# A pointwise convolution streamed through one core: chunks of 2048 rows in four buffers, or of 4096 rows in three

## The chip, the core and the metric

The kernel runs on one core of one Trainium2 chip. The metric is the device time in microseconds (us) of one execution; the time of a version is the median of its runs. A profile is one execution on the chip, recorded by the hardware profiler. The engines are called PE (matmul), PEld (its weight loads), DVE (VectorE), ACT (ScalarE), POOL (GpSimd) and SP (which here only issues DMAs and waits).

## What is computed

The reference is a depthwise separable convolution with a 1 x 1 depthwise part, on an image of 384 x 384 pixels with 384 channels, all in bf16:

```python
H = W = 384; C = 384; k = 1
out = x * dw[0, 0]                        # one factor per channel
return einsum('bhwc,cd->bhwd', out, pw)   # 384 x 384 matrix
```

With one row per pixel this is a matrix product: 147,456 rows of 384 values, times a 384 x 384 matrix whose rows have been scaled by `dw`. The input and the output have 113.2 MB each.

## The kernel before

**Tiling.** The work is cut into 288 supertiles of 512 rows. Supertiles are gathered in chunks, and a chunk is what one load and one store move. `_chunks` makes chunks of 1, 1 and 2 supertiles at the start, then 70 chunks of `LMAX` = 4 supertiles (2048 rows), then 2, 1 and 1 at the end: 76 chunks. Chunk t uses input buffer `Xs[t % NX]` and output buffer `Os[t % NO]`, with four of each.

**Layout.** A load gives each of the 128 partitions 4L consecutive rows of a chunk of L supertiles, so that its run in memory is 4L x 768 bytes: 12 KB for L = 4. A supertile j of the chunk takes four of these rows per partition, L rows apart (the view `(k l)` in `transposes`). A store writes four runs per partition, one for each quarter q of the chunk, of L rows each: 3 KB for L = 4. At any L a load has one run per partition and a store four.

**One supertile.** DVE transposes its rows into `Ts` in two instructions (line 174), each over 96 pairs of channels. PE multiplies with 48 small matmuls (line 134) on four row groups into a PSUM buffer of four banks. Then the result is evicted to the output buffer with a cast to bf16: DVE takes quarter 3 (line 212) and ACT takes quarters 0 to 2 (line 215). `Ts` and the PSUM buffers are double, so supertiles alternate between two of each. The scaled weights `w_r` are made once at the start, by DVE and ACT.

**Order.** Everything is written out by hand and tied by semaphores. DVE's order in the main loop is: evict supertile jj, then transpose supertile jj + 2. PE runs a loop over pairs of supertiles. DVE waits for a chunk's load before the chunk's first transposes (`s_x`), and both DVE and ACT wait, before a chunk's first eviction, for the store that last used the output buffer (`s_o`).

**SP's queue.** All loads of x and all stores are issued on SP, in one order: the first NX loads, and then for each t, load t + NX and store t. Load t + NX waits for the last transposes of chunk t, since these free the input buffer (line 95). Store t waits for the last evictions of chunk t by DVE (line 105) and by ACT (line 107). An instruction that waits on SP holds up those behind it.

Of the kernel before, what the change touches and what calls it, by code (L numbers as in the profile page):

```python
# [9 lines left out]
U32 = mybir.dt.uint32  # L10
COPY = mybir.ActivationFunctionType.Copy

LMAX = 4
NX = 4
NO = 4


def _chunks(n_super: int):

    head, tail = [1, 1, 2], [2, 1, 1]  # L20
    mid = n_super - sum(head) - sum(tail)
    assert mid > 0 and mid % LMAX == 0
    return head + [LMAX] * (mid // LMAX) + tail


@with_exitstack
def kernel(
# [22 lines left out]

    NS = N // 512
    chunks = _chunks(NS)
    NT = len(chunks)
    s0 = [sum(chunks[:t]) for t in range(NT)]
# [11 lines left out]

    Xs = [bufp.tile([P, 4 * LMAX, C], BF16, name=f"X{i}") for i in range(NX)]
    Ts = [bufp.tile([P, NB, 256], BF16, name=f"T{i}") for i in range(2)]
    Os = [bufp.tile([P, 4 * LMAX * D], BF16, name=f"O{i}") for i in range(NO)]
    PS = [psum.tile([P, 4, 512], F32, name=f"ps{s}") for s in range(2)]  # L70

    s_x = [nc.alloc_semaphore(f"s_x{i}") for i in range(NX)]
    s_t = [[nc.alloc_semaphore(f"s_t{i}{h}") for h in range(2)] for i in range(2)]
    s_pe = nc.alloc_semaphore("s_pe")
    s_a = [nc.alloc_semaphore(f"s_a{i}") for i in range(2)]
    s_d = [nc.alloc_semaphore(f"s_d{i}") for i in range(2)]
    s_o = [nc.alloc_semaphore(f"s_o{i}") for i in range(NO)]
    s_dw = nc.alloc_semaphore("s_dw")
# [5 lines left out]
    with tc.tile_critical():  # L84
# [6 lines left out]
        def load_x(t):  # L91
            L = chunks[t]
            r = 512 * s0[t]
            src = xf[r : r + 512 * L, :].rearrange("(p s) c -> p (s c)", p=P)
            d = nc.sync.dma_start(Xs[t % NX][:, : 4 * L, :].rearrange("p s c -> p (s c)"), src)  # L95
            if t >= NX:
                je = s0[t - NX] + chunks[t - NX] - 1
                d._wait_ge(s_t[je % 2][1], je // 2 + 1)
            d.then_inc(s_x[t % NX], 16)

        def store(t):
            L = chunks[t]
            r = 512 * s0[t]
            je = s0[t] + L - 1
            nc.sync.wait_ge(s_d[je % 2], je // 2 + 2)
            dst = of[r : r + 512 * L, :].rearrange("(q p j) d -> p q (j d)", q=4, p=P)
            d = nc.sync.dma_start(dst, Os[t % NO][:, : 4 * L * D].rearrange("p (q e) -> p q e", q=4))
            d._wait_ge(s_a[je % 2], je // 2 + 2)
            d.then_inc(s_o[t % NO], 16)

# [9 lines left out]
        for t in range(NT):  # L120
            if t + NX < NT:
                load_x(t + NX)
            store(t)
        for o in range(NO):
            nc.sync.wait_ge(s_o[o], 16 * len(range(o, NT, NO)))

# [123 lines left out]
```

## Time and profile before

| | before |
|---|---|
| median of 8 runs | 588.48 us (587.54 to 590.28) |
| the profiled execution | 590.12 us, with a span of 588.3 us from its first to its last instruction |
| granted PE clock | 0.994 |
| busy in the span | PE 564.3, DVE 564.1, PEld 396.7, ACT 326.7 us |
| HBM traffic | read 114.43 MB, written 113.25 MB, 387 GB/s over the span |
| queue of SP's DMAs | 51,488 packets, 227.09 MB, 98.5% of 16 DMA engines' time |
| loads of 1.5 MB | 70, median 13.8 us from issue to landing |
| stores of 1.5 MB | 70, median 15.5 us from issue to landing |

A row of the profile's list of groups is to be read so: line, engine, operation, destination and source with shapes, the count, the busy time in us and the mean in ns of one, and at last the idle time of the engine before such instructions, with what ended most of it. "To landing" is the time from the issue of a DMA until its last byte has arrived and its semaphore is raised. It holds the time in which the DMA lies in the queue behind others. The share of the DMA engines is a mean over 16 of them.

### The profile page before, as it was taken

Reading aid. Unit: us, or ns where it says so; the run is one execution under the profiler, and the core shown is the slowest. Engines: PE = TensorE matmul, PEld = TensorE weight load, DVE = VectorE, ACT = ScalarE, POOL = GpSimd, SP = SyncE. Lnnn points to the kernel's source line nnn. Section 1 sums busy time; section 2 is a strip of 40 time slices with the busy share of each in tenths; the row PEclk is TensorE's granted clock in tenths of the full one; section 3 lists DMA queues with packets and bytes.
Section 4 is the critical chain, followed back from the end, with each engine's and each line's share of the span. In section 5 each row is a group of like instructions: output and inputs, shape, how many; then the busy total and the mean of one; then the engine's idle time right before and its main releaser. Section 6 shows DMA issues by size and latency. Waiting matters only on the chain.

```text
span 588.3 us, 30055 instructions
## 1 busy us (share of the span) xinstructions
PE 564.3 (96%) x13824; PEld 396.7 (67%) x13824; DVE 564.1 (96%) x876; ACT 326.7 (56%) x297; POOL 0.3 (0%) x5
## 2 busy tenths in 40 slices
PE   1999999999999999999999999999999999999992
PEld 0677777777777777777777777777777777777771
DVE  3899999999999999999999999999999999999991
ACT  3455555555555655555555556555555555565552
POOL 0000000000000000000000000000000000000000
PEclk9999999999999999999999999999999999999997
DMA  8999999999999999999999999999999999999974
GB/s 293 348 407 407 406 402 411 387 390 416 403 399 394 402 401 404 395 385 419 416 403 395 399 396 401 415 420 413 404 396 390 391 406 376 395 386 374 374 300 168
DMA packets 52126, 227.81 MB, mean 387 GB/s; under 512 B 2704, under 2 KB 6544, under 8 KB 43152
## 3 DMA queue, kind: packets, MB, share of 16 engines
q1 hardware_dynamic: 51488, 227.09, 98.5%
q10 hardware_dynamic: 624, 0.59, 0.4%
q14 instruction: 13, 0.11, 0.1%
q8 instruction: 1, 0.02, 0.0%
HBM read 114.43 MB, written 113.25 MB: 387 GB/s over the span
## 4 chain that ended last, share of the span: by engine, by line
PE 93%; DMA 4%; ACT 1%; SPq 0%; issue 0%; ACTq 0%
PE ps L134 93%; DMA out_dram<-O 3%; DMA pw_r<-in_pw_dram 1%; ACT w_r L199 1%; ACT O L215 0%; SPq L89 0%; SPq L95 0%; SPq L245 0%; ACTq L211 0%; ACTq L194 0%; SPq L84 0%
## 5 line engine op out<-in xcount | busy, mean ns | idle before, releaser
L134 PE MATMUL ps<-w_r,T 32*128 32x384 bf16 x13824 | 564.3, 322 | 14.1 <-ACT w_r L199 13.0
L134 PEld LDWEIGHTS ps<-w_r,T 32*128 32x128 bf16 x13824 | 396.7, 93 | 181.4 <-issue 14.5
L215 ACT CAST O<-ps 128x1152 bf16<-128x1152 f32 x288 | 322.0, 1118 | 245.8 <-PE ps L134 242.8
L174 DVE STREAM_TRANSPOSE T<-X 128x384 uint32<-128x384 uint32 x576 | 448.0, 853 | 1.5 <-PE ps L134 1.4
L212 DVE CAST O<-ps 128x384 bf16<-128x384 f32 x288 | 160.7, 558 | 7.1 <-PE ps L134 5.0
L199 ACT ACTIVATE w_r<-pw_r,dwsel 128x384 bf16<-128x384 bf16 x6 | 3.1, 601 | 5.7 <-DMA pw_r<-in_pw_dram 5.7
L186 DVE CAST dwsel<-dwt 32x12 f32<-32x12 bf16 x4 | 0.7, 164 | 3.7 <-DMA dwt<-in_dw_dram 3.6
L197 DVE TENSOR_SCALAR w_r<-pw_r,dwsel 128x384 bf16<-128x384 bf16 x6 | 1.5, 312 | 2.6 <-DMA pw_r<-in_pw_dram 2.6
L160 ACT ACT_TABLE_LOAD x1 | 1.3, 1283 | 2.3 <-issue 2.3
L157 DVE MEMSET seed<- 128x1 f32 x2 | 0.1, 59 | 1.0 <-SPq L84 1.0
L160 ACT COPY warm<-warm 128x1 f32<-128x1 f32 x2 | 0.3, 188 | 0.0
L234 POOL MEMSET const-uint8-127<- 128x1 uint8 x1 | 0.1, 102 | 0.0
L234 POOL MEMSET const-bfloat16-1.0<- 128x1 bf16 x1 | 0.1, 101 | 0.0
L158 POOL MEMSET warm<- 128x3 f32 x1 | 0.1, 100 | 0.5 <-SPq L84 0.5
L234 POOL MEMSET const-float32-0.0<- 128x1 f32 x1 | 0.1, 98 | 0.2 <-issue 0.2
L234 POOL MEMSET const-float32-1.0<- 128x1 f32 x1 | 0.1, 98 | 0.0
## 6 DMA issues: line engine op xcount, KB each, us to landing
X<-in_x_dram SPq DMA_DIRECT2D x70, 1536.0 KB, 13.8
out_dram<-O SPq DMA_DIRECT2D x70, 1536.0 KB, 15.5
X<-in_x_dram SPq DMA_DIRECT2D x4, 384.0 KB, 11.6
X<-in_x_dram SPq DMA_DIRECT2D x2, 768.0 KB, 14.9
out_dram<-O SPq DMA_DIRECT2D x4, 384.0 KB, 7.0
out_dram<-O SPq DMA_DIRECT2D x2, 768.0 KB, 9.8
pw_r<-in_pw_dram ACTq DMA_DIRECT2D x2, 288.0 KB, 5.9
pw_r<-in_pw_dram SPq DMA_DIRECT2D x2, 288.0 KB, 6.6
```

Of the source, the lines that this page charges most:

```text
L134: mm = nc.tensor.matmul(PS[s][:, q, :D], lhsT=Ts[s][32 * q : 32 * q + 32, b, par::2], rhs=w_r[32 * q : 32 * q + 32, b, par, :], start=(b = ...
L157: nc.vector.memset(seed[:, s : s + 1], 0.0).then_inc(s_d[s])
L158: nc.gpsimd.memset(warm[:], 0.0).then_inc(s_seed)
L160: c = nc.scalar.copy(warm[:, s + 1 : s + 2], warm[:, 0:1])
L174: ins = nc.vector.transpose(out=Tw[:, 3 * h : 3 * h + 3], in_=Xw[:, :, j, 96 * h : 96 * h + 96].rearrange("p k (b w) -> p b k w", w=32),)
L186: nc.vector.tensor_copy(dwsel[32 * q : 32 * q + 32, :], dwt[:].rearrange("w b r -> w (b r)")).then_inc(s_ds)
L197: i = nc.vector.tensor_scalar_mul(w_r[:, b, r, :], pw_r[:, b, r, :], sc)
L199: i = nc.scalar.activation(w_r[:, b, r, :], pw_r[:, b, r, :], COPY, scale=sc)
L212: e = nc.vector.tensor_copy(Ov[:, 3, j, :], PS[s][:, 3, :D])
L215: a = nc.scalar.copy(Ov[:, 0:3, j, :], PS[s][:, 0:3, :D])
L234: nc = _bacc.Bacc("TRN2", target_bir_lowering=False, num_devices=1)
```

## The change

Chunks become twice as large and buffers fewer: `LMAX` goes from 4 to 8, so that a chunk has 4096 rows, and there are three input and three output buffers in place of four. One more step of 4 supertiles is put into the start and the end, so the chunks are 1, 1, 2, 4, then 34 of 8, then 4, 2, 1, 1: 42 chunks. A full load has 3 MB with a run of 24 KB per partition, and a full store has four runs of 6 KB per partition. The buffers of each kind hold 24 supertiles together, where they held 16.

```diff
-LMAX = 4
-NX = 4
-NO = 4
+LMAX = 8
+NX = 3
+NO = 3
 
 def _chunks(n_super: int):
 
-    head, tail = [1, 1, 2], [2, 1, 1]
+    head, tail = [1, 1, 2, 4], [4, 2, 1, 1]
     mid = n_super - sum(head) - sum(tail)
     assert mid > 0 and mid % LMAX == 0
     return head + [LMAX] * (mid // LMAX) + tail
```

On PE, DVE and ACT the instructions and their order stay as they are, with other buffers behind them. On SP there are 42 loads of x and 42 stores in place of 76 and 76. Load t + 3 now follows the freeing of chunk t's buffer, where it was load t + 4.

## The prediction

> **What bounds the kernel now.** I read the page's costliest groups first, then the timeline around one supertile (512 rows), then the landing times of the DMAs in stretches, and last the stretches at the end. The groups name two full engines:
>
> ```profile
> L134 PE MATMUL ps<-w_r,T 32*128 32x384 bf16 x13824 | 564.3, 322 | 14.1 <-ACT w_r L199 13.0
> L174 DVE STREAM_TRANSPOSE T<-X 128x384 uint32<-128x384 uint32 x576 | 448.0, 853 | 1.5 <-PE ps L134 1.4
> L212 DVE CAST O<-ps 128x384 bf16<-128x384 f32 x288 | 160.7, 558 | 7.1 <-PE ps L134 5.0
> ```
>
> PE's ends are modelled, so its 564.3 decides nothing. DVE's columns are busy total, mean ns, idle before: with 1.5 and 7.1 us of idle in all, DVE runs without a gap. The timeline gives its beat:
>
> ```profile
> 27.34 0.56 DVE L212 CAST O<-ps 128x384 bf16<-128x384 f32 x1
> 27.34 1.12 ACT L215 CAST O<-ps 128x1152 bf16<-128x1152 f32 x1 [0.83 <-PE ps L134]
> 27.81 1.55 DVE L174 STREAM_TRANSPOSE T<-X 128x384 uint32<-128x384 uint32 x2
> 29.29 0.56 DVE L212 CAST O<-ps 128x384 bf16<-128x384 f32 x1
> ```
>
> One eviction and two transposes, 29.29 - 27.34 = 1.95 us per supertile. Supertile 0's pair, before PE had started, took 1.54 us too, so this is DVE's own time. Eviction j starts at 21.49 + 1.95 (j - 2), so the last (287) is due at 577.24. It started at 579.38. The loss is at the end, and the DMAs make it. Loads, columns as in the page (issue durations min/median/max; then us to landing), in the stretches 50 to 100, 450 to 500 and 500 to 540 us:
>
> ```profile
> L95 SPq DMA_DIRECT2D X<-in_x_dram x7: 328/328/328, 52.8 to 99.6; - x7
> DMA to landing us min/median/max: 8.2/9.3/9.7
> ...
> L95 SPq DMA_DIRECT2D X<-in_x_dram x7: 328/349/1176, 450.6 to 497.4; - x7
> DMA to landing us min/median/max: 18.4/18.8/19.9
> ...
> L95 SPq DMA_DIRECT2D X<-in_x_dram x5: 328/2825/3951, 505.2 to 536.4; - x5
> DMA to landing us min/median/max: 20.6/22.1/22.3
> ```
>
> Same transfers, same spacing, and each lands later: a backlog grows. From 100-150 (median 10.6) to 450-500 (18.8) it is 8.2 us in 350, or 0.18 us per chunk of 7.8: the DMAs need 7.98 us where DVE takes 7.8. It is one engine of the 16 (columns: DVE and ACT busy, granted clock, DMA share, GB/s):
>
> ```profile
> 568.00:570.00 2.00, 2.00 (x56) 1.40 (x52) 2.00 (x5) 1.17 (x2) 0.00 (x0) 1.00 0.22 85
> 570.00:571.00 1.00, 1.00 (x33) 0.69 (x25) 1.00 (x2) 0.55 (x1) 0.00 (x0) 1.00 0.07 25
> 583.00:584.00 1.00, 0.00 (x0) 0.00 (x0) 0.00 (x0) 0.00 (x0) 0.00 (x0) 0.50 0.07 25
> ```
>
> A share of 0.07 is one sixteenth. At 570 fifteen engines have finished everything issued, and one still works on a load (issued 559.79, landing 15.4 later at 575.2) and a store (562.78, landing 16.5 later at 579.3). The transposes of supertile 287 start at 575.33, with that load (the view names PE for it). The last eviction starts at 579.38, with that store.
>
> **What can be won.** Without backlog: last ScalarE eviction 577.24 + 1.12 = 578.4, a store like the first one (3.7 us to landing) 582.1, and the 1.3 us from the last landing (580.5 + 6.5 = 587.0) to the span's end: 583.4. So of the span of 588.3 at most 4.9 us can go. The rest is DVE's beat: the change issues the same 864 compute instructions on DVE in the same order, and leaves ScalarE's and PE's order alone. X is read at another stride (row groups 6 KB apart, not 3 KB). Supertile 0 (768 B apart) took 1.54 us a pair and the others 1.55, so I cost it at nothing.
>
> **Part by part.**
> *DMA count and run length.* 76 loads and 76 stores become 42 and 42; on each DMA engine, 8 load runs of 12 KB and 32 store runs of 3 KB per 2048 rows become 8 of 24 KB and 32 of 6 KB per 4096. What a run costs shows at the end, where the slow engine is alone: stores land at 579.3, 583.0, 584.9, 585.9 with 98.3, 49.2 and 24.6 KB per engine for the last three intervals. 3.7 - 1.0 us for 73.7 KB more is 27.3 GB/s, and 1.0 us less 24.6 KB at that rate leaves 0.1 us for 32 runs: about 3.1 ns a run. Twenty runs saved per 7.8 us are 0.06 us. The backlog's growth falls from 0.18 to 0.12 per 2048 rows, 0.24 per new chunk; 34 chunks give 8.2 us.
> Is more saved? 3.146 MB at 16 x 27.3 GB/s are 7.20 us, so 0.78 us per pair of DMAs are above it. If that sits at the turn from load to store and back, the change halves it (-0.39 us, no backlog at all); if it goes with the bytes on that one engine, only the 0.06 is saved. Bounds 0.06 to 0.39, and none if longer runs bring a cost of their own. I take 0.06: at 570, without turns and without other engines, the one engine moved 25 GB/s, so most of its slowness goes with bytes.
> Two rules of the Trainium skill, page "DMA: Bandwidth & Descriptors", stand against the rows. Section "Where 436 GB/s comes from" says that for HBM to SBUF transfers the HBM side binds at about 358 GB/s. By it longer runs can't help and this kernel would take 227.8 MB / 358 = 636 us; the page shows 387 to 420 GB/s in most slices, so I drop it. Section "Anatomy of one DMA" fits some 2.0 us fixed per DMA (for the other issue path): 68 fewer DMAs would save 136 us. The row allows 0.78 us for two, since queued DMAs overlap, and all but 4.9 us is behind DVE anyway.
> *Slack.* A load is issued when its buffer's last transposes end, and needed NX - 1 chunks on: 3 x 7.8 = 23.4 us before, 2 x 15.6 = 31.2 after. The new load itself takes some 7.3 us and the store 8.5, so base landing times rise by about 7.5, the same as the slack. No stall in mid-run unless the backlog passes about 12 us. On SP a load that waits for its buffer has that chunk's own store behind it, which waits for evictions two supertiles later anyway, so the longer wait holds nothing up.
> *Head.* Before, loads 4 (issued 7.0), 5 (18.72) and 6 (21.59) fed supertiles 8 to 19. Now chunk 4 (supertiles 8 to 15, 3 MB) waits for chunk 1's buffer and, on SP, behind the first store: issue 18.7. Its rows are due at 29.76. Before, half of it took 8.4 us to land (27.1); load 4 of the same size landed 3.6 us after load 3. So 27.1 + 3.6 = 30.7, a stall of 1.0 us. Bounds: 0 (if the slow 8.4 was a start effect) to 4.3 (both halves slow). I take 1.0. It moves all of DVE's work.
> *Tail.* The last load (supertile 287) now waits for chunk 38's transposes, issued at about 567.6 instead of 559.8, and lies in SP's queue and the rings behind the 3 MB store of chunk 37, issued 562.8. Queue empty by then: first packet about 1.5 us after issue, 8.5 for the store on the slow engine, 0.9 for the load: 573.7, due at 573.8. No stall, no reserve. The store of chunk 38 (570.6) follows at +4.3 = 578.0; its buffer is due at 577.24: 0.8 us. Is the queue empty? In the two chunk periods before 562.8 the loads are 1.5, 0.8 and 0.4 MB instead of 3 and 3: 3.6 + 4.6 = 8.2 us are given back against 8.2 of backlog. It just is.
> *Sum.* Last eviction 577.24 + 1.0 + 0.8 = 579.0, ScalarE 580.2, last store 4.0 (it follows small ones), 1.3: span 585.5, 2.8 under 588.3. The profiled execution took 590.12, 1.8 around its span; the median of 588.48 is 1.6 lower, so an ordinary run probably has a little less tail to win. I take 2.5: 586.0.
>
> **Rivals.**
> *Forecast, 0.47: 586.0.*
> *The turns were the cost, 0.12: 584.3.* Growth gone, tail wait gone, only the head's 1.0 left: 583.4 + 1.0, which is 3.9 under the span, 0.3 less for the median. For it: loads alone at 11 to 18 us ran at 393 to 449 GB/s. Against it: 25 GB/s at 570 without turns.
> *Gain given back, 0.16: 588.5.* Between 500 and 540 the landing rose 3.3 us more, beyond the steady growth, with 360 to 385 GB/s. If such a patch comes again, the queue isn't empty at 562.8 but 3.3 behind, and the last load is late by that much: 585.5 + 3.3 = 588.8, half a us over the span, which the median's smaller tail takes back.
> *Slower, 0.25: 591.3.* The last load behind the 3 MB store. If longer runs save the slow engine nothing, 0.36 us per chunk x 34 = 12.2, less 8.2 given back, leaves 4.0, or 7.3 with such a patch; each us delays the last transposes one for one: span 589.5 to 592.8, the middle 2.9 over the span before. It decides from a remainder of 2.8 us. For it: the reserve there is 0.1 us, where the old tail issued that load 7.8 us earlier. Against it: the 3.1 ns per run.
> About 0.2% is what can be told from no change here: faster 0.59, same 0.16, slower 0.25. The range: 583.6 (all 4.9 us) to 592.0 (most of the slower case).
>
> **What would show it.** Transposes still 853 ns and evictions 1.95 us apart; load landings rising from about 15 by 5 to 8 us, not by 14; a DVE idle of about 1 us before supertile 8 at 30 us; the last load issued near 568 and landing near 574 to 576; a last eviction near 579. It is wrong if landings rise past 30 us (waits on stores in mid-run, slower), if they don't rise at all (second case), or if the head stalls by 3 us or more.

## The result, and the profile after

The changed kernel takes 586.82 us (median of 22 runs, 585.83 to 587.37) where the kernel before takes 588.21 (59 runs). The ratio is 0.9969 (95% interval 0.996 to 0.9977), that is 1.8 us of 588; the two medians are 1.4 apart. The forecast was 586.0, 2.5 us less than before. Ratios here and below are of fast runs alone: three of the 22 runs of e3, its profiled execution among them, are slow, at 596.8 us and more with a granted clock of 0.987 to 0.989. The profiled execution took 585.49 with a span of 583.7, which is at the fast end: the other runs have spans of 583.1 to 585.6, most near 585.0.

DVE's beat of 1.95 us is as it was. The landing times of the loads are not. The same view as before (issue durations min/median/max on SP, then us to landing), for the stretches 100 to 150, 450 to 500 and 500 to 530 us of the changed kernel:

```profile
L95 SPq DMA_DIRECT2D X<-in_x_dram x3: 327/328/328, 107.6 to 138.8; - x3
DMA to landing us min/median/max: 15.3/15.5/15.7
...
L95 SPq DMA_DIRECT2D X<-in_x_dram x4: 327/328/328, 450.8 to 497.6; - x4
DMA to landing us min/median/max: 19.2/19.4/19.5
...
L95 SPq DMA_DIRECT2D X<-in_x_dram x2: 327/328/328, 513.2 to 528.8; - x2
DMA to landing us min/median/max: 16.1/17.8/19.6
```

Two things are to be seen. The landing rises by 3.9 us in 350, or 0.17 per chunk of 15.6 us, where it had risen 0.18 per 7.8: the growth is halved. And after 500 there is no jump: the full load issued at 513.2 lands after 19.6 us, where before the change the median rose to 22.1. (The load at 528.8, 16.1, is already one of half the size.) The middle number of the issue line is the one I had printed and not read. It stays at 328 ns here; before the change it was 2,825 ns in the stretch 500 to 540. An issue that took a third of a microsecond took three.

The start shows the forecast stall before supertile 8 (timeline of DVE):

```profile
28.91 0.56 DVE L212 CAST O<-ps 128x384 bf16<-128x384 f32 x1
30.24 1.55 DVE L174 STREAM_TRANSPOSE T<-X 128x384 uint32<-128x384 uint32 x2 [0.77 <-DMA X<-in_x_dram]
31.66 0.53 DVE L212 CAST O<-ps 128x384 bf16<-128x384 f32 x1
```

At the end, the stretches (DVE and ACT busy, clock, DMA share, GB/s) show the one slow DMA engine again, here catching up before the last 3 MB store. The timeline shows the last load issued late and the last eviction waiting:

```profile
556.00:558.00 2.00, 2.00 (x56) 1.50 (x52) 2.00 (x5) 1.15 (x2) 0.00 (x0) 1.00 0.06 22
558.00:560.00 2.00, 2.00 (x56) 1.47 (x51) 2.00 (x5) 1.17 (x2) 0.00 (x0) 1.00 0.07 25
```

```profile
563.02 0.39 SPq L107 DMA_DIRECT2D out_dram<-O  x1
...
567.83 0.33 SPq L95 DMA_DIRECT2D X<-in_x_dram  x1
...
575.52 0.56 DVE L212 CAST O<-ps 128x384 bf16<-128x384 f32 x1
578.28 0.56 DVE L212 CAST O<-ps 128x384 bf16<-128x384 f32 x1 [2.20 <-DMA out_dram<-O]
```

The load landed 6.1 us after its issue, at 573.9, and was due at 574.05. Of the 2.20 us of idle before the last eviction 0.8 are lost: 2 x 1.95 after the eviction at 573.57, it was due at 577.47.

### The profile page after: what moved, and what is told of

Same layout as the page of the kernel before. It is cut to its first block, busy times and chain, and to the rows that moved or that the text cites. A ratio compares the mean times of both kernels' runs of the same rounds, so it can differ in the third digit from the quotient of the medians.

```text
span 583.7 us, 29852 instructions
## 1 busy us (share of the span) xinstructions
PE 564.2 (97%) x13824; PEld 415.9 (71%) x13824; DVE 563.9 (97%) x876; ACT 326.7 (56%) x297; POOL 0.3 (0%) x5
## 4 chain that ended last, share of the span: by engine, by line
PE 93%; DMA 5%; ACT 1%; SPq 0%; issue 0%; DVE 0%; ACTq 0%; DVEq 0%
PE ps L134 93%; DMA X<-in_x_dram 2%; DMA out_dram<-O 1%; DMA pw_r<-in_pw_dram 1%; ACT O L215 1%; ACT w_r L199 1%; DVE T L174 0%; SPq L89 0%; SPq L107 0%; SPq L95 0%; SPq L245 0%; DVEq L173 0%; ACTq L211 0%; ACTq L194 0%; SPq L84 0%
## 5 line engine op out<-in xcount | busy, mean ns | idle before, releaser
L134 PEld LDWEIGHTS ps<-w_r,T 32*128 32x128 bf16 x13824 | 415.9, 93 | 161.1 <-issue 13.5
```

Of the source, the lines that this page charges most:

```text
L134: mm = nc.tensor.matmul(PS[s][:, q, :D], lhsT=Ts[s][32 * q : 32 * q + 32, b, par::2], rhs=w_r[32 * q : 32 * q + 32, b, par, :], start=(b = ...
```

## The experiments

Each group of experiments has its own runs of the kernel before; the ratio with its interval is to those.

| run | median us | before, same group | ratio (95%) |
|---|---|---|---|
| e1 3 KB store runs | 589.19 | 589.26 | 0.9996 (0.9974 to 1.0018) |
| e2 twice the turns | 587.93 | 589.26 | 0.9977 (0.9961 to 0.9993) |
| e3 before, six buffers | 592.09 | 589.26 | 1.0038 (1.0014 to 1.0061) |
| e4 changed, fourth input buffer | 584.54 | 589.26 | 0.9915 (0.9884 to 0.9945) |
| e5 changed, again | 586.42 | 589.03 | 0.9956 (0.9941 to 0.9972) |
| e6 smoother start | 585.14 | 589.03 | 0.9933 (0.9912 to 0.9954) |
| e7 smoother end | 586.65 | 589.03 | 0.9949 (0.9933 to 0.9965) |
| e8 before, stores on ACT | 586.05 | 589.03 | 0.9956 (0.9937 to 0.9975) |
| e9 before, six buffers, stores on ACT | 592.34 | 587.97 | 1.0066 (1.0043 to 1.009) |
| e10 before, a quarter of the matmuls | 557.67 | 587.97 | 0.9483 (0.9463 to 0.9504) |

**e1: short store runs put back.** The edit, on the changed kernel:

```diff
+            parts = 2 if L == LMAX else 1
+            w = L * D // parts
+            for h in range(parts):
+                d = nc.sync.dma_start(dst[:, :, h * w : h * w + w], o_v[:, :, h * w : h * w + w])
+                d.then_inc(s_o[t % NO], 16)
```

> The changed kernel, but every full store goes out as two DMAs, one for each half of a run: 3 KB runs again, 64 instead of 32 per DMA engine and chunk, next to each other in the queue. Loads, buffers and chunks as in the changed kernel. Theory (each run has a fixed price of about 3 ns on the slow DMA engine, and the growing backlog decides the end): 32 x 3.1 = 0.10 us more per chunk, so load landings grow by 0.27 instead of 0.17 us per 15.6 us, some 3 us more backlog at the end, the last load late: time about 1 to 3 us above the changed kernel (587.5 to 590). Rival (the turn between loads and stores is what costs, and is as frequent as in the changed kernel): growth 0.17, time 586.8. Rival (the gain is from deeper buffers): 586.8.

No gain is left that the runs can tell: 0.9996 (0.9974 to 1.0018). The landing rises from a median of 16.0 (100 to 150) to 21.6 (450 to 500), 0.25 per 15.6 us, against 0.27 expected. And the long issues are back, here in the stretch 450 to 500:

```profile
L95 SPq DMA_DIRECT2D X<-in_x_dram x4: 352/1350/2824, 450.7 to 497.5; - x4
L115 SPq DMA_DIRECT2D out_dram<-O x6: 372/631/3729, 453.7 to 485.7; - x6
```

So the store's run length carries the gain; buffers, chunks and load runs alone don't. Two things come back together here, the price of each run and the long issues, and this run doesn't separate them. The 34 stores more than in the changed kernel are not the main reason: e2 has as many, and more loads too, and keeps half of the gain or more.

**e2: turns put back.** Loads and stores in halves, queued alternately:

```diff
+            for h in range(2) if chunks[t] == LMAX else [None]:
+                if t + NX < NT:
+                    load_x(t + NX, h)
+                store(t, h)
```

> The changed kernel, but full loads and stores are cut in two (loads in half runs of 12 KB, stores in two quarters each with runs of 6 KB) and queued alternately: half load, half store, half load, half store. As many turns between loading and storing per row as before the change, but only 8 short runs more per DMA engine and chunk. Theory (price per run): growth of load landings 0.17 + 8 x 0.003 = 0.20 us per 15.6 us, time within 1 us of the changed kernel. Rival (price per turn): growth back to 0.3 or more per 15.6 us, so 4 us more backlog and 588.5 or more.

1.3 us under the kernel before: of a gain of 0.0031 in the ratio (0.0044 in e5) 0.0023 stays (interval 0.0007 to 0.0039). The later halves land after a maximum of 15.0 at 100 to 150 and 20.0 at 450 to 500: 0.22 per 15.6 us, near the 0.20 of the theory. A small price per turn isn't excluded; as the main cost it is out.

**e3: depth alone.** `NX = 6`, `NO = 6` in the kernel before.

> The kernel before with six buffers of each kind in place of four: 24 supertiles of buffering as after the change, but chunks, runs and DMA count as before. Theory (runs): load landings still grow by 0.18 us per 7.8 us. The six loads at the start fill the queue earlier, which takes 1 to 2 us off the end: 586 to 587.5. Rival (the gain came from the depth alone, and short runs cost nothing): growth clearly under 0.18 per 7.8 us, and the time of the changed kernel or less.

Both expectations missed: it is slower than before. The profiled execution took 597.28, above the median, at a granted clock of 0.987, so its stretches are stronger than the ordinary run's. Issues and landings of loads and stores in the stretch 300 to 350, with the page's GB/s row:

```profile
L95 SPq DMA_DIRECT2D X<-in_x_dram x7: 327/3831/6449, 301.9 to 349.0; - x7
DMA to landing us min/median/max: 22.7/25.1/26.4
L107 SPq DMA_DIRECT2D out_dram<-O x6: 827/942/3361, 305.0 to 347.5; - x6
```

```profile
GB/s 289 421 411 418 421 421 423 420 421 422 422 411 390 385 416 415 413 389 369 398 349 382 361 366 379 362 384 350 402 362 400 375 397 378 390 390 349 352 395 105
```

Up to about 170 us, with the queue always full of data, the DMAs move 420 GB/s, and from there to 250 about 404, which is what DVE takes (3.146 MB per 7.8 us are 403). From about 260 us on the issues take microseconds and the rate sinks below that, to 350 to 400 in most slices. That gave a new theory: a queue holds a limited number of runs per DMA engine. Once the slow engine's part is full, an issue waits for it, and the other fifteen get no more work than it does. An estimate of the limit: with 40 runs per 7.8 us and a landing of 20 us (250 to 300, where e3's issues begin to lengthen), about 103 runs wait; in the kernel before it begins at a landing of 19.8, so at 102. The estimate is on the high side. If one counts instead the slow engine's runs of DMAs that haven't landed when a long load issue ends, there are about 85, the load's own 8 included, in the kernel before, in e3 and in e10. The changed kernel, with 40 runs per 15.6 us, comes by the same estimate to 64 at its largest landing of 25.0.

The trace bears out what the fifteen do. Each DMA raises its semaphore in 16 steps, one per DMA engine, so the trace has the time of the slow engine and of the fifteenth. In the kernel before, the slow one finishes its part of a load a median of 1.0 us after the fifteenth at 60 to 150, 8.8 at 450 to 500, and then, while issues are long, the distance stays at about 10: the fifteen no longer draw ahead. One thing isn't explained. The slow engine has DMAs waiting all the time, and yet it gets slower too: in the kernel before its loads land 8.0 us apart up to 517 and 8.4 from there to 551, in e3 8.0 and then 8.3. In the kernel before this makes some 1.4 us.

**e4: a fourth input buffer.** `NX = 4` in the changed kernel.

> The changed kernel with a fourth input buffer (NX = 4, NO = 3). The first 3 MB load is then issued at about 7 us, not at 18.5, and the last load at about 560, ahead of the 3 MB store. Theory (after the change what is left is a head stall of 0.8 us and the queue at the end): no idle of DVE before supertile 8, no late last load, and DMA work done earlier: 584.5 to 586, that is 1 to 2 us under the changed kernel. Rival (what is left is DVE's beat and fixed ends): 586.5 to 587.

The best version: 584.54, with spans of 582.5 to 583.2. DVE has no idle time before supertile 8, but waits 1.1 us at 34.1 for a store to free an output buffer; a fourth one of these was not tried. The last load goes out ahead of the 3 MB store, and the last eviction waits for PE alone:

```profile
560.51 0.33 SPq L95 DMA_DIRECT2D X<-in_x_dram  x1
563.48 15.97 SPq L107 DMA_DIRECT2D out_dram<-O  x5
```

```profile
577.94 0.56 DVE L212 CAST O<-ps 128x384 bf16<-128x384 f32 x1 [1.39 <-PE ps L134]
```

**e5: the changed kernel again**, beside e6 to e8.

> The changed kernel once more, as the measure for the runs beside it: 0.997 of the kernel before, load issues on SP 0.33 us each to the end, and no stretch under 380 GB/s before the last loads.

As expected, with a ratio a little lower. In this profile DVE's stall before supertile 8 is 1.55 us, twice the first one's:

```profile
30.54 0.86 DVE L174 STREAM_TRANSPOSE T<-X 128x384 uint32<-128x384 uint32 x1 [1.55 <-DMA X<-in_x_dram]
```

**e6: a smoother start.**

```diff
-    head, tail = [1, 1, 2, 4], [4, 2, 1, 1]
+    head, tail = [1, 1, 2, 4, 4, 4], [4, 2, 1, 1]
```

> The changed kernel with chunks of 1, 1, 2, 4, 4, 4 at the start, so that supertiles 8 to 11 come with a 1.5 MB load. Theory (the stall of DVE before supertile 8 moves all that follows): the stall of 0.8 us goes and the time falls by 0.5 to 0.8 us against the changed kernel. Rival (the end hangs on the queue, not on DVE): no change, within 0.3 us.

1.3 us under e5, more than the 0.5 to 0.8 expected, in line with e5's stall of 1.55. DVE runs through without idle at supertile 8. The head stall is real and moves the end by most of its length.

**e7: a smoother end.**

```diff
-    head, tail = [1, 1, 2, 4], [4, 2, 1, 1]
+    head, tail = [1, 1, 2, 4], [4, 4, 4, 2, 1, 1]
```

> The changed kernel with chunks of 4, 4, 4, 2, 1, 1 at the end, so that no 3 MB store goes out at 563 and the store of the last shared output buffer has less in front of it. Theory (last eviction waits 0.8 us for a store behind the 3 MB store and the last load): the wait goes, 0.5 to 1 us less than the changed kernel. Rival (last stores' own landing sets the end): no change, within 0.3 us.

Nothing within 0.3 us, as the rival had it, though not for its reason. The wait only moved: the last load is issued at 568.7 and lands after 6.9 us. By their semaphores fifteen engines have delivered it after 3.4 us (6.0 in the changed kernel, where the sixteenth needs 6.1), so fewer bytes lie ahead of it, but the slow engine still has its backlog.

```profile
575.71 1.56 DVE L174 STREAM_TRANSPOSE T<-X 128x384 uint32<-128x384 uint32 x2 [0.68 <-DMA X<-in_x_dram]
...
579.84 0.56 DVE L212 CAST O<-ps 128x384 bf16<-128x384 f32 x1 [2.18 <-DMA out_dram<-O]
```

**e8: two queues for the short runs.** In the kernel before, the stores go to ACT's queue:

```diff
-            d = nc.sync.dma_start(dst, Os[t % NO]...)
+            d = nc.scalar.dma_start(dst, Os[t % NO]...)
...
-            store(t)
...
+            if j == L - 1:
+                store(t)
```

> The kernel before (chunks of 2048 rows, four buffers) with the stores issued on ACT's queue, after ACT's last eviction of the chunk, so that loads and stores lie in two queues, each with half of the runs or less. Theory (what costs most before the change is that about 110 runs per DMA engine fill the one queue at 500 us: SP's issues then take 3 to 5 us and the rate falls from about 400 to 370 GB/s): SP's load issues stay at 0.33 us and the rate holds to the end: 585.5 to 587.5. Rival (only the price of each run and the slow engine count): the backlog at the end is as before, 588 to 589.5.

As the theory had it: 3 KB runs, 76 DMAs each way, four buffers, and the same 0.9956 as e5. Loads and stores in the stretch 450 to 500:

```profile
L95 SPq DMA_DIRECT2D X<-in_x_dram x7: 328/328/328, 451.4 to 498.2; - x7
DMA to landing us min/median/max: 9.0/9.3/9.8
L107 ACTq DMA_DIRECT2D out_dram<-O x6: 378/378/378, 454.4 to 493.4; - x6
DMA to landing us min/median/max: 23.8/24.1/24.3
```

No long issue, and 406 GB/s from 500 to 540 where the kernel before had 383. But this run changes more than the full queue. Loads no longer lie behind stores, and land after 9.3 us where they took 18.8. And the slow engine, whose backlog now lies in the stores (landing 13.1 at 60 to 150, 24.1 here), falls behind less. These 11.0 us more are, at 32 runs of some 137 ns per 7.8 us, about 6 us of its work; in the kernel before it was 9.0 over the same time. Six evictions of ACT wait 8.2 us in all for their buffer. So the run agrees with the full queue as a cost of its own, beside the price of the runs, but doesn't show what it is worth.

**e9: depth and two queues.**

> The kernel before with six buffers of each kind, and the stores on ACT's queue. With six buffers and one queue it took 592 us, with SP's issues at 3 to 7 us and 370 GB/s from 300 us on. Theory (the number of runs waiting in one queue is what costs): loads and stores in two queues stay under the limit for longer, SP's issues stay near 0.33 us and the rate near 405 GB/s: 584.5 to 587. Rival (more data in flight slows the DMAs by itself, whatever the queue): 590 or more, with 370 to 385 GB/s in the second half.

Missed: 592.34. SP's issues stayed at 0.33 us as expected, but with six buffers the stores' backlog grows to a landing of 30 us, which is 32 x 30 / 7.8 = 123 runs on ACT's queue alone by the estimate (101 to 111 counted, the waiting issue's own 32 included), and the limit shows there. ACT must then stand still with its evictions behind the issue. The chain that ended last:

```profile
528.38 1.13 ACT O L214
529.53 3.62 ACTq L107
533.15 0.04 issue
533.21 0.04 issue
533.25 1.13 ACT O L214
```

3.62 us for an issue that takes 0.38 otherwise, and PE and DVE behind it. Five such issues lie on this chain, 13.8 us in all. My assumption that the two queues stay under the limit was wrong; the limit itself appears a second time, at a like count. The rival's numbers came true as well: over 590 us, and 383 and 381 GB/s at 450 to 540. Against its reason stands that the same six buffers ran at 405 and 401 GB/s from 100 to 450, until ACT's issues lengthened, and e10, below.

**e10: whose work slows the one engine.** In the kernel before, 36 of the 48 matmuls of a supertile are left out, so three quarters of the products are missing from the output:

```diff
+                        if (b, par) not in ((0, 0), (2, 1), (5, 1)):
+                            continue
```

> The kernel before with 12 of the 48 matmuls of each supertile; the other 36, three quarters of the products, are left out. DVE, ACT, loads and stores are as they were, so DVE's beat of 1.95 us should stay. Theory (the one slow DMA engine is slow through PE's work or its instructions, since its store runs speed up when PE ends): landings no longer grow by 0.18 us per 7.8 us, and the time goes to 584.5 to 586. Rival (the slow engine is slow through the traffic of DVE and ACT, or by itself): growth and time as before, 588 to 589.5.

The time fell far below both, because the beat of DVE itself fell. Its two groups in e10:

```profile
L176 DVE STREAM_TRANSPOSE T<-X 128x384 uint32<-128x384 uint32 x576 | 436.1, 831 | 2.1 <-DMA X<-in_x_dram 2.1
L214 DVE CAST O<-ps 128x384 bf16<-128x384 f32 x288 | 155.1, 538 | 5.9 <-DMA out_dram<-O 2.3
```

They were 853 and 558 ns. The evictions follow each other by 1.82 to 1.83 us up to 350, not 1.95 (the shorter instructions make up only half of the difference), and then by about 1.9, with ACT waiting for stores. The DMAs move 411 to 427 GB/s from the second slice to the fourth from the end:

```profile
GB/s 281 420 411 423 418 418 416 421 423 423 426 425 418 423 422 421 423 422 425 423 423 422 420 422 424 424 425 423 422 420 421 423 424 422 427 422 421 406 360 153
```

And that with a full queue, here at 450 to 500:

```profile
L95 SPq DMA_DIRECT2D X<-in_x_dram x7: 328/4862/5785, 451.7 to 497.7; - x7
```

So a full queue alone doesn't lower the rate. Here no engine is far behind: the last one finishes a load at most 2.4 us after the fifteenth.

The landing growth can't be compared, since the demand rose with the beat. The store runs themselves can: in the trace's packet records of the kernel before some 5.5% of the 3 KB runs, about one engine in sixteen, lie above 124 ns with a mean of about 138, where the others take 121. In e10 only 2% do, with a mean of 131. The full queue isn't the reason: e3 at 60 to 150, at 422 GB/s, has 5.5%. So PE's work slows that engine, in the profiled executions at least. By which path isn't shown; the profiler too has less to record in e10, 9,319 instructions instead of 30,055.

## Why the prediction was right, and where it was not

**The end, not the beat: right.** The floor of 583.4 for the span was nearly right: e4 has spans of 582.5 to 583.2. The last store took 2.9 us to land in the changed kernel, not the 3.7 of the floor or the 4.0 of the sum.

**"This is DVE's own time": wrong.** e10 shows that the beat of 1.95 depends on PE's load: with a quarter of the matmuls it is 1.82 to 1.83. Supertile 0's pair at 1.54 us agreed by chance or by a cause not tried. The change leaves PE alone, so nothing in the sum hung on it.

**Run length: right in kind, too small in size.** I took 0.06 us per 2048 rows as saved, so a growth of 0.24 per chunk; it was 0.17, a saving of 0.10 per 2048 rows. e1 puts 0.04 of it back with store runs alone. The 3.1 ns a run came from landings rounded to 0.1 us. In the packet records two 3 KB runs of the slow engine take 2 x 138 ns and one of 6 KB takes 267.6, which is 8 ns less; and runs that follow each other overlap by 3 to 4 ns, so one run fewer saves 4 to 5. Twenty of these are 0.09 us. That most of the slowness goes with bytes is confirmed by the same numbers.

**The turns: not the cost.** e2 has them back and keeps half of the gain or more. That case was also added up wrongly: 3.6 us under 588.48 is 584.9, not 584.3.

**The slow patch at 500 to 540: the step that failed.** I took it for a chance event that might come again (the case "gain given back", 0.16). Its size was misread, too: the 3.3 us from 18.8 to 22.1 are the whole rise, and steady growth makes 1.1 of them. e3 and e9 show that it goes with the full queue: issues of 2 to 7 us, and 368 to 383 GB/s in the mean of a stretch. The changed kernel and e8 have none of it, so the change takes it away. What this is worth alone was not measured; the slow engine's later landings, some 1.4 us, are the nearest figure. The same line of the profile that gave me the landing carried the sign, 328/2825/3951.

**Slack: right.** No wait for a load or a store in mid-run, at landings up to 25.0.

**Head: right in kind, 1.0 forecast.** Measured 0.77 and 1.55 in two profiles, and 1.3 in time by e6.

**Tail: right.** The last load landed at 573.9 (forecast 573.7), the last eviction lost 0.8 (forecast 0.8). "It just is" empty was true: at 558 to 560 only one engine was still at work. But e7 shows that the size of the last big store isn't all that counts: without it, the slow engine's backlog held the last load as long.

**The size: 1.8 us by the ratio, 2.5 forecast.** That runs saved more than I took, and that the patch went too, adds little: the forecast already had the queue empty before the last load, and behind that stands DVE's beat. The profile of before (590.12) was one of the longer runs and that of after one of the shortest, so the pair shows 4.6 us. What the change leaves over e4 is 2.3 us (586.82 against 584.54, measured at different times); by e6 more than half of that is the head. A head stall taken at 1.5 instead of 1.0 would have brought the sum to 2.0.

**Slower, 0.25:** it needed longer runs to save nothing. e1, where the store's runs don't get longer, shows the last load late as that case had it (DVE waits 2.76 us for it at 576.7), and ends level with the kernel before, not 3 us above.

## What to carry to other kernels

Read landing times in stretches, not as one median: a steady rise says that the DMAs are slower than the engines, long before any engine waits. Read the issue durations beside them. Here issues of microseconds went with a queue full of runs, and then fewer and longer runs (the change) or a second queue (e8) helped, while more buffers made it worse, in one queue (e3) and in two (e9). When chunks get larger, one more buffer on the input side can pay for the late loads at both ends, as it did here (e4).

## What had not been expected of the hardware

An issue blocked when some 85 runs per DMA engine waited in SP's queue (counted, its own included: the kernel before, e3, e10) or 101 to 111 in ACT's (e9), and the blocked issue held its whole instruction stream: 3.62 us of ACT in e9. With one slow engine and a full queue the rate fell from the 403 GB/s that DVE takes to between 350 and 400 (e3), and the slow engine itself became slower; with a full queue and little work on PE the DMAs kept 420 (e10). DVE's instructions took 2.6 and 3.6% less time when PE did a quarter of its work.
